# Attention and a three-way maxout layer on one core: the planner that orders all instructions gets new durations and lags

## The chip, the cores and the metric

One core of a Trainium2 chip runs the whole program. The metric is the device time of one execution in microseconds (us). A core has five engines with instruction queues of their own: TensorE (PE, matrix products; PEld in the profile is its loading of weights), VectorE (DVE), ScalarE (ACT), GpSimd (POOL) and SyncE (SP, which here only issues DMAs). Each engine takes its instructions strictly in the order in which they stand in its queue; an instruction that has to wait for another engine holds everything behind it.

## The reference

```python
def _attn_ref(q, k, v):                    # (8, 8, 576, 64) each
    scores = (1 / 8) * np.matmul(q, k.transpose(0, 1, 3, 2))
    mask = (pos[:, None] // 64) >= (pos[None, :] // 64)
    scores = np.where(mask, scores, -1e9)
    scores = scores - np.max(scores, axis=-1, keepdims=True)
    attn = np.exp(scores)
    attn = attn / (np.sum(attn, axis=-1, keepdims=True) + 1e-09)
    return np.matmul(attn, v)

def _moe_ref(x, w1, w2, w3, w_out):        # x: (4608, 512), w1..w3: (512, 768), w_out: (768, 512)
    h = np.maximum(np.maximum(x @ w1, x @ w2), x @ w3)
    return h @ w_out
```

So: attention over 8 batches of 8 heads with a mask in blocks of 64, its heads put side by side as the rows of x, three products of x with 512x768 matrices, their maximum, and a product with a 768x512 matrix, all in 32-bit floats.

## The kernel before

**Tiling.** Attention goes by pairs of heads: 4 pairs a batch. Batch 0 is cut in two parts, FRONT (queries 0 to 255) and BACK (the rest), so that its first results come early; the 28 pairs of batches 1 to 7 are whole. A pair needs: q and k loaded (tile nat, L875 and L893), turned (L824 on PE for batch 0, one DVE transpose L917 of 1152 columns for the others), scores on PE (L933, and L940 for the last 64 queries of both heads together), mask and row maximum in one DVE instruction (L422), exponential with row sum on ACT (L606, L960), reciprocal of the sum on DVE (L746, L750, L971, L977), normalising on ACT or POOL (L438, L440), turning the probabilities (PE L558 and L986 with copies for batch 0; for the others DVE L629 and L633 and then SP's DMAs L641, eight a pair), and the product with v (L1000). The result x is split in a rounded part xh (ACT, L249) and a remainder xl (POOL, L254), since the following products (L1118) work on 32-bit numbers in three steps: xh by the upper part of the weight, xl by the upper, xh by the lower. Each batch's x is one chunk of 256 columns and one of 320. A chunk takes 18 groups of 4 x 3 such products, the maximum on DVE (L1133), and then the output products L1184.

**Weights.** The 24 blocks of 512 columns ("units": 18 of w1 to w3, then 6 of w_out) are split into upper and lower part during the first 149 us. A unit is a DMA by POOL (L292), |w| on ACT (L302), five DVE operations in a row (L308, L315, L321, L327, L338; the first, second and fourth read one tensor, the other two read two), a rounding copy on ACT, three products on PE that add up what is left ("the whole": L345, L346, L347), and a copy back on ACT. There is one tile "left" that L338 writes and L347 reads.

**What sets the order.** The kernel first makes a list of jobs. A job has a rank, predecessors, buffers it takes and gives, and for each engine that could do it an assumed duration. `in_order` then plays this list through: at each moment an idle engine starts the ready job of lowest rank; a job becomes ready a lag (table LAG) after the last predecessor ends on another engine; buffers count. A job that two engines could do goes to whichever takes it first. The sequence so obtained is the order in which instructions are written to the queues of all engines, so assumed durations decide the order on each engine, and for some jobs the engine, but nothing else: the instructions themselves and their waits are the same.

The durations come from `pe`, `dve`, `act`, `pool` (functions of the columns), `norm_cost` (normalising), `RAISE` (a turn of 128 columns on PE), `SMALL` (a reciprocal or a sum of a few columns), and from sums of these in `Unit.__init__`, `Head.plan` and `Pair.plan4`; `GAP` is the time between two dependent DVE operations. DMA times (`SEND`, `LOAD`, `ASK`, `DMA`, `MOVE`, `TURNED`) are constants too.

Of the kernel before, what the change touches and what calls it, by code (L numbers as in the profile page):

```python
# [23 lines left out]
EPS = 1e-9  # L24


TO_PE = 250.0
LAG = {
    "PE": {"PE": 0.0, "ACT": 200.0, "DVE": 200.0, "POOL": 200.0, "SP": 200.0},
    "ACT": {"PE": TO_PE, "ACT": 0.0, "DVE": 90.0, "POOL": 160.0, "SP": 150.0},  # L30
    "DVE": {"PE": TO_PE, "ACT": 130.0, "DVE": 0.0, "POOL": 155.0, "SP": 150.0},
    "POOL": {"PE": TO_PE, "ACT": 130.0, "DVE": 130.0, "POOL": 0.0, "SP": 150.0},
    "SP": {"PE": 100.0, "ACT": 100.0, "DVE": 100.0, "POOL": 100.0, "SP": 0.0},
}
SEND = 620.0
# [3 lines left out]
MOVE = 4500.0  # L39
TURNED = 4400.0  # L40

GAP = 60.0
SMALL = 130.0

RAISE = 215.0
DEBUG = False


# [89 lines left out]
def pe(*cols, least=128):  # L138
    return sum(max(n, least) / 2.4 + 13.5 for n in cols)


def dve(n, fast=False):
    return 100.0 + n / (1.92 if fast else 0.96)


def act(n, psum=True):
    return (105.0 if psum else 135.0) + n / 1.2


def pool(n):  # L150
    return 120.0 + 2.6 * n


@with_exitstack
def kernel(
# [29 lines left out]
    TURN = 12  # L185
# [53 lines left out]
    def job(cost, rank, call, *args, after=(), take=(), give=(), lasts=0.0, moved=0.0):  # L239
        j = Job(cost, rank, lambda eng: call(eng, *args), after, take, give, lasts, moved)  # L240
        jobs.append(j)
        return j

    def join(after, give):
        return job({}, 0, lambda eng: None, after=after, give=give)
# [11 lines left out]
    class Unit:  # L257


        def __init__(self, u, src, dst, n, prior, *early, first=None):  # L260
            self.src, self.dst, self.n, self.u = src, dst, n, u
            self.last = n == DO
            rank = DELAY + PACE * u


            self.tag = f"wo{dst}" if self.last else f"w{u}"
            self.temps = (f"wo{u % NF}",) if not self.last else (f"wo{4 + dst % 2}",) if dst < 4 else ("osb", "osb")
            j = self.issued = job(
                {"POOL": ASK},
                rank - 8,  # L270
                self.load,
                after=(prior and prior.issued, first, *(e.sized for e in early if e)),
                take=(self.tag,) if self.last else (),
            )
            j = job({}, 0, lambda eng: None, after=(j,), lasts=MOVE, moved=1600.0)
            j = self.sized = job({"ACT": act(512, False)}, rank, self.size, after=(j,), take=self.temps)
            for step, fast in (
                (self.clamp, True),
                (self.shift, True),
                (self.sign, False),  # L280
                (self.power, True),
                (self.rest, False),
            ):
                c = dve(512, fast)
                j = job({"DVE": c}, rank, step, after=(j,), take=("left",) if step == self.rest else (), lasts=c + GAP)
            j = job({"ACT": act(512, False)}, rank, self.high, after=(j,))
            j = job({"PE": 6 * pe(512)}, rank, self.whole, after=(j,), take=("pm",), give=(*self.temps, "left"))
            self.done = job({"ACT": act(512)}, rank, self.lower, after=(j,), give=("pm",))
# [142 lines left out]
        return t.rearrange("p (k j r) -> p k j r", j=4, r=r)  # L431

    def norm_cost(n):
        return {"POOL": 160.0 + 1.86 * n, "ACT": 235.0 + n / 1.2}

    def normalise(eng, p, r):
        if eng == "ACT":
# [4 lines left out]
    class Head:  # L442
# [7 lines left out]
        def plan(self, t0):  # L450

            pair, part, self.exps, self.inv = self.pair, self.pair.part, {}, {}
            for n, ts in enumerate(part.groups):
                apart, r = None, t0 + (SECOND if part.beside and ts == part.later else n)
                for t in ts:
                    m = P * (t + 1)
                    d = job(
                        {"DVE": dve(m) + 120.0},
                        r + 1,
                        self.top,  # L460
                        t,
                        after=(pair.scored[ts], apart, pair.began),
                        take=("stat",) if pair.began is None else (),
                    )
                    pair.began = pair.began or d
                    if t != ts[-1]:
                        apart = job({}, 0, lambda eng: None, after=(d,), lasts=GAP)
                    self.exps[t] = job({"ACT": act(m) + 240.0}, r + 2, self.exp, t, after=(d,), take=(f"p{t}",))
                join([self.exps[t] for t in ts], BANK)

        def turns(self, t0, after):
# [9 lines left out]
            if part.last:  # L481
                first = job({"DVE": dve(512) + dve(128)}, t0 + 11, self.turn, 4, after=(pair.scaled, after), take=("pz",))
                self.turned = [first]
# [22 lines left out]
        def plain_turns(self, t0):  # L506
# [19 lines left out]
            for t in part.tiles:  # L526
                up = job(
                    {"PE": RAISE * (t + 1)},
                    t0 + 12,
# [8 lines left out]
            if part.last:  # L538
                if self.j == 0:
                    pair.raised = [  # L540
                        job({"PE": RAISE * n}, t0 + 12, pair.raise4, a, after=(pair.scaled, gate), take=("sb",))
                        for a, n in ((0, 4), (1, 1))
# [100 lines left out]
    BANK = ("sb", "sb5", "scores")  # L643

    class Pair:
# [12 lines left out]
        def plan(self, first, before):  # L658
# [67 lines left out]
            for r, ts in ((first + 7, [t for g in part.first for t in g]), (first + SECOND + 5, part.later)):  # L726
                if ts:
                    r = r if ts != part.later or part.beside else first + 8
                    cols = slice(min(COL[t] for t in ts), max(COL[t] for t in ts) + 1)
                    exps = [h.exps[t] for h in self.heads for t in ts]  # L730
                    inv = job({"DVE": SMALL}, r, self.sum, cols, after=exps, lasts=SMALL + GAP)
                    inv = job({"DVE": SMALL}, r, self.inverse, cols, after=(inv,))
                    for h in self.heads:
# [16 lines left out]
            nc.vector.reciprocal(rs[:, :, c], rs[:, :, c])  # L750

        def plan4(self, first, tq, last):
            asked = job({"ACT": 2 * act(64, False)}, first - TURN + 2, self.ask, after=(tq,), take=("q8",))
            tops = []
            for a in range(2):
                last = job({"PE": 4 * pe(64 if a else 512)}, first + 3 + a, self.qk4, a, after=(asked, last), take=BANK)
                tops.append(
                    job(
                        {"DVE": dve(64 if a else 512) + 120.0},
                        first + 4 + a,  # L760
                        self.top4,
                        a,
                        after=(last, *tops),
                        take=() if a else ("stat4",),
                    )
                )
            e = job({"ACT": act(512) + act(64) + 480.0}, first + 5, self.exp4, after=tops, take=("p4",), give=2 * BANK)
            inv = job({"DVE": SMALL}, first + 6, self.sum4, after=(e,), lasts=SMALL + GAP)
            inv = job({"DVE": SMALL}, first + 6, self.inverse4, after=(inv,))
            self.scaled = job(norm_cost(S), first + 7, self.scale4, after=(inv,), give=("stat4",))  # L770
            join((last,), ("q8",))
            return last
# [12 lines left out]
        def plain_qk(self, rank, loads):  # L785
# [13 lines left out]
            for n, (chunks, copies) in enumerate(banks):  # L799
                up = job(  # L800
                    {"PE": RAISE * len(chunks)},
                    rank,
# [5 lines left out]
                ) if n == 0 else job(  # L808
                    {"PE": RAISE * len(chunks)}, rank, self.raise_qk, n, chunks, after=(ups[0], loads["kn"], loads["qn"]), take=("sb", "sb5")
                )  # L810
# [28 lines left out]
        def finish(self, prior, r, priors={}):  # L839
            self.xjobs = {}  # L840
            for half in self.part.halves:
                n = HALF[half]
                done = job(
                    {"ACT": act(n), "DVE": dve(n)},
                    r + 2,
                    self.out,
                    half,
                    after=(priors.get(half, prior),),
                    take=(f"x32_{half}",),
                    give=("sb",),  # L850
                )
                h = job({"ACT": act(n, False)}, r + 4, self.x_high, half, after=(done,), take=(f"xh{half}",))
                self.xjobs[half] = job(
                    {"POOL": pool(n)}, r + 4, self.x_low, half, after=(h,), take=(f"xl{half}",), give=(f"x32_{half}",)
                )
            join((prior,), (self.tag,) * self.part.loads + ("vn",))
# [168 lines left out]
    left = {}  # L1025

    class Chunk:


        def __init__(self, b, half, pairs, prior, start, end):  # L1030
# [13 lines left out]
            for f in range(NF):  # L1044
                ev = None
                for i in range(3):
# [19 lines left out]
                    )  # L1066
                h = job({"ACT": act(256, False)}, NOW, self.high, f, after=(ev,), take=(f"hh{f}",))
                l = job({"POOL": pool(256)}, NOW, self.low, f, after=(h,))
                self.done[f] = [l]
                if spare:  # L1070
# [152 lines left out]
    rank = 0  # L1223
# [54 lines left out]
```

## Time and profile before

| what | us |
|---|---|
| three runs: median, lowest, highest | 927.47, 925.59, 927.82 |
| the profiled execution: time, span | 927.53, 925.7 |
| PE busy | 895.4 (97% of the span) |
| DVE busy | 530.1 (57%) |
| ACT busy | 479.6 (52%) |
| POOL busy | 246.3 (27%) |
| products L1118 on the chain that ended last | 49% of the span |
| output products L1184 on it | 16% |

A busy share is an average over the whole span; the windows below show it by stretch. A PE instruction's length in the profile contains a modelled end that overlaps the next one, so what an instruction costs PE is read from the distance of two starts, or from a run of equal ones on the chain of waits. The same holds for DVE and ACT, whose next instruction starts a little before the one ahead ends.

### The profile page before, as it was taken

What the parts mean: (1) busy time and instruction counts of PE and PEld (TensorE: products, weight loads), DVE (VectorE), ACT (ScalarE), POOL (GpSimd) and SP (SyncE); (2) the same over time, 40 slices, a digit from 0 to 9 for tenths busy, and PEclk for the clock granted to TensorE, in tenths of its full rate; (3) what the DMA queues carried; (4) which work ended last, traced back from release to release, by engine and by line L of the source; (5) the groups of instructions that cost most, each with busy time, mean ns of one, the idle gap of its engine ahead of it and who ended that gap; (6) DMA issues with size and microseconds to landing.
All of it is one profiled execution on the core that took longest, in us unless ns stands there. A gap on an engine that the chain in (4) does not pass through costs nothing.

```text
span 925.7 us, 16909 instructions
## 1 busy us (share of the span) xinstructions
PE 895.4 (97%) x5880; PEld 744.7 (80%) x5880; DVE 530.1 (57%) x1555; ACT 479.6 (52%) x1359; POOL 246.3 (27%) x377
## 2 busy tenths in 40 slices
PE   6798899999999999999999999999999999999998
PEld 4456667886988888888888888888888888899997
DVE  4999688786674655465574655465664655431101
ACT  3777557655564555556464555555464654522111
POOL 3522232333231222223132222223131322222101
PEclk9999999999999999999999999999999999999999
DMA  6841535576644554555533555555543543330010
GB/s 197 232 144 54 125 85 126 127 141 145 131 94 100 113 123 105 133 110 124 118 86 80 114 123 107 123 111 132 110 99 75 115 113 84 95 73 24 1 35 23
DMA packets 226132, 98.36 MB, mean 106 GB/s; under 512 B 189696, under 2 KB 218368, under 8 KB 226048
## 3 DMA queue, kind: packets, MB, share of 16 engines
q1 hardware_dynamic: 208192, 82.35, 40.3%
q0 software_dynamic: 3456, 12.58, 4.0%
q10 hardware_dynamic: 14400, 2.36, 1.4%
q8 instruction: 46, 0.75, 0.3%
q14 instruction: 38, 0.31, 0.1%
HBM read 41.94 MB, written 9.44 MB: 56 GB/s over the span
## 4 chain that ended last, share of the span: by engine, by line
PE 90%; DVE 5%; ACT 1%; issue 1%; DMA 1%; POOL 1%; ACTq 0%; SPq 0%; DVEq 0%; POOLq 0%
PE pm L1118 49%; PE pm L1184 16%; PE sb L1000 10%; PE sb L933 9%; PE sb L940 3%; PE pm L345 1%; DVE sb L422 1%; DVE wo L321 1%; DVE wo L308 1%; DVE left L338 1%; POOL p L440 1%; DMA nat<-in_q_dram 1%; PE sb L558 0%; ACT w L249 0%; DVE wo L315 0%
## 5 line engine op out<-in xcount | busy, mean ns | idle before, releaser
L1118 PE MATMUL pm<-xh,w 128*128 128x320 f32 (+1 forms) x2304 | 500.2, 304 | 0.7 <-ACT w L249 0.7
L1118 PEld LDWEIGHTS pm<-xh,w 128*128 128x128 f32 x2304 | 379.9, 190 | 20.1 <-issue 15.3
L1118 PE MATMUL pm<-xl,w 128*128 128x256 f32 (+1 forms) x1152 | 341.2, 296 | 0.7 <-POOL xl L254 0.5
L1118 PEld LDWEIGHTS pm<-xl,w 128*128 128x128 f32 x1152 | 219.0, 190 | 7.2 <-issue 5.3
L422 DVE CUSTOM_DVE_ANT_0 sb<-sb,mask 128x512 f32<-128x512 f32 (+3 forms) x288 | 144.8, 529 | 138.3 <-PE sb L940 70.0
L1133 DVE TENSOR_TENSOR m<-pm,m 128x256 f32<-128x256 f32 (+1 forms) x192 | 87.3, 455 | 167.1 <-PE pm L1118 159.0
L606 ACT ACTIVATE p<-sb,nm 128x128 f32<-128x128 f32 (+3 forms) x256 | 134.2, 528 | 75.0 <-DVE nm L422 62.8
L254 POOL TENSOR_TENSOR hl<-m,hh 128x256 fp32r<-128x256 f32 x96 | 71.6, 746 | 316.9 <-ACT hh L249 285.1
L629 DVE STREAM_TRANSPOSE pz<-p 128x512 f32<-128x512 f32 (+1 forms) x280 | 136.4, 525 | 21.8 <-ACT p L438 20.0
L440 POOL TENSOR_TENSOR p<-p,rs 128x384 f32<-128x384 f32 (+4 forms) x129 | 90.0, 719 | 186.7 <-DVE rs L750 180.8
L1184 PE MATMUL pm<-wo,hh 128*128 128x512 f32 x384 | 119.2, 391 | 0.0
L249 ACT CAST hh<-m 128x256 fp32r<-128x256 f32 x96 | 39.0, 406 | 121.3 <-DVE m L1133 120.7
L438 ACT ACTIVATE p<-p,rs 128x512 f32<-128x512 f32 (+4 forms) x159 | 89.6, 608 | 20.2 <-DVE rs L750 12.9
L1000 PE MATMUL sb<-pt,vn 128*64 128x320 f32 (+4 forms) x840 | 90.4, 362 | 4.0 <-ACT p L606 2.5
L254 POOL TENSOR_TENSOR xl<-x,xh 128x256 fp32r<-128x256 f32 (+1 forms) x64 | 51.9, 815 | 156.1 <-ACT xh L249 150.0
L933 PE MATMUL sb<-kq 64*128 64x256 f32 (+3 forms) x512 | 88.5, 466 | 2.6 <-DVE kq L251 2.0
L1000 PEld LDWEIGHTS sb<-pt,vn 128*64 128x64 f32 x840 | 55.3, 137 | 37.4 <-issue 5.0
L1184 PEld LDWEIGHTS pm<-wo,hh 128*128 128x128 f32 x384 | 71.0, 188 | 15.1 <-issue 0.3
L933 PEld LDWEIGHTS sb<-kq 64*128 64x128 f32 x512 | 45.5, 192 | 38.1 <-issue 21.7
L1184 PE MATMUL pm<-wo,hl 128*128 128x512 f32 x192 | 74.8, 390 | 0.0
L249 ACT COPY m<-pm 128x256 f32<-128x256 f32 (+1 forms) x96 | 38.3, 399 | 45.9 <-PE pm L1118 33.3
L249 ACT COPY osb<-pm 128x512 f32<-128x512 f32 x36 | 21.1, 587 | 75.7 <-PE pm L1184 75.7
(82 smaller groups left out, 762.5 us busy)
## 6 DMA issues: line engine op xcount, KB each, us to landing
pt<-pz SPq DMA_DIRECT2D x224, 200.0 KB, 3.9
w<-in_moe_w_dram POOLq DMA_DIRECT2D x18, 512.0 KB, 5.6
vn<-in_v_dram SPq DMA_DIRECT2D x64, 128.0 KB, 2.4
out_dram<-osb SPq DMA_DIRECT2D x32, 256.0 KB, 2.1
nat<-in_k_dram SPq DMA_DIRECT2D x112, 72.0 KB, 2.3
nat<-in_q_dram SPq DMA_DIRECT2D x96, 72.0 KB, 2.7
wo<-in_moe_w_out_dram POOLq DMA_DIRECT2D x6, 512.0 KB, 4.2
nat<-in_q_dram ACTq DMA_DIRECT2D x16, 72.0 KB, 3.2
```

The lines of the kernel that those rows point to most:

```text
L249: nc.scalar.copy(dst, src)
L254: {"DVE": nc.vector, "POOL": nc.gpsimd}[eng].tensor_tensor(out=dst, in0=a, in1=b, op=ALU.subtract)
L422: nc.vector.tensor_tensor_reduce(out=ps, in0=ps, in1=hidden, scale=-SCALE, scalar=first, op0=ALU.add, op1=ALU.min, accum_out=out_)
L438: nc.scalar.mul(p, p, r)
L440: nc.gpsimd.tensor_tensor(out=p, in0=p, in1=r.broadcast_to([P, p.shape[1]]), op=ALU.mult)
L606: nc.scalar.activation(dst, src, AF.Exp, bias=nm[:, c : c + 1], scale=-1.0, accum_out=sm[:, c : c + 1])
L629: nc.vector.transpose(dst, p[:, 0 : n * P])
L933: nc.tensor.matmul(ps, self.q[h.own, P * t : P * (t + 1)], self.k[h.own, 0:w], start=True, stop=True)
L1000: nc.tensor.matmul(o[h.own].rearrange("p (i u) -> p i u", u=n)[:, :, c0 : c0 + z - a], self.vn[:, kt, h.j, :], h.pt[:, :, h.off + a : h.of ...
L1118: nc.tensor.matmul(self.ps, w[i, f][:, c, :], xx, start=(c == 0 and s == 0), stop=(c == NC - 1 and s == 2))
L1133: nc.vector.tensor_tensor(out=m, in0=ps, in1=m, op=ALU.max)
L1184: nc.tensor.matmul(self.po[: self.rows], h, w[f], start=(f == 0 and s == 0), stop=(f == NF - 1 and s == 2))
```

## The change

New numbers in the planner, none in the instructions. The core of the diff:

```diff
-TO_PE = 250.0
+TO_PE = 180.0
-    "ACT": {"PE": TO_PE, "ACT": 0.0, "DVE": 90.0, "POOL": 160.0, "SP": 150.0},
-    "DVE": {"PE": TO_PE, "ACT": 130.0, "DVE": 0.0, "POOL": 155.0, "SP": 150.0},
-    "POOL": {"PE": TO_PE, "ACT": 130.0, "DVE": 130.0, "POOL": 0.0, "SP": 150.0},
+    "ACT": {"PE": TO_PE, "ACT": 0.0, "DVE": 140.0, "POOL": 180.0, "SP": 150.0},
+    "DVE": {"PE": TO_PE, "ACT": 120.0, "DVE": 0.0, "POOL": 240.0, "SP": 150.0},
+    "POOL": {"PE": TO_PE, "ACT": 90.0, "DVE": 130.0, "POOL": 0.0, "SP": 150.0},
-GAP = 60.0
-SMALL = 130.0
-RAISE = 215.0
+GAP = 85.0
+SMALL = 100.0
+RAISE = 110.0
 def dve(n, fast=False):
-    return 100.0 + n / (1.92 if fast else 0.96)
+    return 68.0 + n / (1.92 if fast else 0.96)
 def act(n, psum=True):
-    return (105.0 if psum else 135.0) + n / 1.2
+    return (52.0 if psum else 88.0) + n / 1.2
 def pool(n):
-    return 120.0 + 2.6 * n
+    return 150.0 + 2.15 * n
...
-                c = dve(512, fast)
+                c = dve(512, fast) + (130.0 if fast else 80.0)
...
-        return {"POOL": 160.0 + 1.86 * n, "ACT": 235.0 + n / 1.2}
+        return {"POOL": 250.0 + 1.5 * n, "ACT": 190.0 + n / 1.2}
...
-                        {"DVE": dve(m) + 120.0},
+                        {"DVE": dve(m) + 35.0},
-                    self.exps[t] = job({"ACT": act(m) + 240.0}, r + 2, self.exp, t, after=(d,), take=(f"p{t}",))
+                    self.exps[t] = job({"ACT": act(m) + 200.0}, r + 2, self.exp, t, after=(d,), take=(f"p{t}",))
```

The durations in `plan4` (L753 to L767) change in the same way. The new file has one line more from L286 on, so its L339 is L338 of before, its L918 is L917, and so on; the text uses the numbers of before.

What this does to the queues: on PE the two orders differ in the first tenth or so and then run through the same sequence of groups, with a few places exchanged; on DVE, ACT and POOL neighbouring instructions change places all the way, and POOL takes 27 normalisations of 512 columns where it took 15, and 11 of 576 where it took 3 (ACT the rest). Three places:

PE, a few rows from the start, where the third and the fourth pair of FRONT are turned (L824) and scored (L933); p_126 and its like are probabilities, pz the turned ones, vn is v. Before:

```order
L933 MATMUL sb<-kq 128x256 x2
L933 MATMUL sb<-kq 128x128 x2
L558 MATMUL sb<-plus,p_139 128x128 x2
L558 MATMUL sb<-plus,p_143 128x128
L824 MATMUL sb<-plus,nat 128x128 x4
L558 MATMUL sb<-plus,p_151 128x128 x2
L558 MATMUL sb<-plus,p_153 128x128
L1000 MATMUL sb<-pz,vn_75 64x256 x2
L1000 MATMUL sb<-pz,vn_75 64x4x32 x2
```

Now, in the same place:

```order
L559 MATMUL sb<-plus,p_126 128x128 x2
L559 MATMUL sb<-plus,p_143 128x128
L559 MATMUL sb<-plus,p_153 128x128
L934 MATMUL sb<-kq 128x256 x2
L934 MATMUL sb<-kq 128x128 x2
L559 MATMUL sb<-plus,p_151 128x128 x2
L1001 MATMUL sb<-pz,vn_75 64x256 x2
L1001 MATMUL sb<-pz,vn_75 64x4x32 x2
L825 MATMUL sb<-plus,nat 128x128 x4
```

The turns of the first pair's probabilities now stand ahead of the third pair's scores, and the first product with v ahead of the fourth pair's turn.

PE, around the 15th unit's whole (w_1024 before and w_1175 now are that unit's weights; kq is the turned q and k). Before, at row 201 of PE's order:

```order
L1118 MATMUL pm<-xl_271,w_697 128x256
L1118 MATMUL pm<-xh_265,w_697 128x256
L345 MATMUL pm<-wo_842,plus 128x512
L346 MATMUL pm<-w_1024,less 128x512
L347 MATMUL pm<-left,plus 128x512
```

Now, at row 256:

```order
L1119 MATMUL pm<-xl_331,w_989 128x256
L1119 MATMUL pm<-xh_326,w_989 128x256
L346 MATMUL pm<-wo_878,plus 128x512
L347 MATMUL pm<-w_1175,less 128x512
L348 MATMUL pm<-left,plus 128x512
L934 MATMUL sb<-kq 128x512 x2
```

Ahead of the 15th whole stand 138 products L1118 where 87 stood, and 26 more turns of 128 columns (L558, L824, L986).

DVE, around the second transpose of a whole pair's q and k (L917); left, w and wo are tiles of the weight units. Before:

```order
L338 SCALAR_TENSOR_TENSOR left<-wo_1179,wo_1264 128x512
L1133 TENSOR_TENSOR m<-pm,m 128x256
L308 TENSOR_SCALAR wo_1327<-wo_1327 128x512
L917 STREAM_TRANSPOSE kq<-nat 128x1152
L971 SCALAR_TENSOR_TENSOR rs_1319<-sm_1318 128x1
```

Now:

```order
L423 ISA sb,nm_1263<-sb,mask,nm_1263 128x64
L423 ISA nm_1263 128x1
L918 STREAM_TRANSPOSE kq<-nat 128x1152
L1134 TENSOR_TENSOR m<-pm,m 128x256
L339 SCALAR_TENSOR_TENSOR left<-w_870,wo_1023 128x512
L972 SCALAR_TENSOR_TENSOR rs_1265<-sm_1264 128x1
```

Before, this transpose stood behind the L338 of the 21st unit, now behind that of the 17th; the first such transpose stands 40 rows ahead of it before and 17 rows now.

## Rows read from the trace of the kernel before

**Rows 1.** Busy time by stretch: window, PE, PEld, DVE, ACT, POOL, clock, DMA, GB/s.
```profile
23.00:93.00 70.00, 59.16 (x317) 37.83 (x314) 66.21 (x163) 53.26 (x137) 25.22 (x33) 0.95 0.49 145
93.00:149.00 56.00, 51.20 (x310) 37.38 (x308) 41.69 (x106) 34.70 (x90) 17.86 (x23) 0.97 0.40 90
149.00:926.00 777.00, 771.03 (x5201) 660.14 (x5199) 411.84 (x1247) 383.06 (x1108) 195.01 (x302) 1.00 0.46 101
```

**Rows 2.** Waits of PE from 93 to 149 us: total, times, longest.
```profile
PE pm L346 <- ACT w L249: 2.7, 1, 2.7
```

**Rows 3.** Waits of DVE in that stretch.
```profile
DVE kq L917 <- DMA nat<-in_k_dram: 3.8, 1, 3.8
```

**Rows 4.** Chain of waits in order of time: start, length, what.
```profile
4.81 1.12 PE sb L824 x4
...
90.12 2.21 PE sb L1000 x20
...
92.87 0.86 PE sb L940 x2
...
95.98 1.07 PE pm L1118 x9
97.05 0.45 PE sb L824 x4
...
149.94 8.16 PE pm L1184 x36
```

**Rows 5.** PE in order of time: start, length, instruction.
```profile
94.95 0.79 PE L346 MATMUL pm<-w,less 128*128 128x512 f32 x1
...
96.89 0.93 PE L824 MATMUL sb<-plus,nat 128*128 128x128 f32 x7
```

**Rows 6.** PE from 207 to 220 us, products of 320 columns and what follows.
```profile
208.30 0.31 PE L1118 MATMUL pm<-xl,w 128*128 128x320 f32 x1
...
208.74 0.31 PE L1118 MATMUL pm<-xl,w 128*128 128x320 f32 x1
...
216.05 2.89 PE L1000 MATMUL sb<-pt,vn 128*64 128x320 f32 x26 [1.50 <-DMA pt<-pz]
218.88 0.70 PE L933 MATMUL sb<-kq 64*128 64x256 f32 x4
```

**Rows 7.** L346 on PE: shortest, median, longest; first and last start.
```profile
L346 PE MATMUL pm<-wo,less x6: 497/796/800, 112.9 to 148.9; 128*128 128x512 f32 x6
```

**Rows 8.** DVE in order of time.
```profile
85.91 0.42 DVE L1133 TENSOR_TENSOR m<-pm,m 128x256 f32<-128x256 f32 x1
...
88.38 0.69 DVE L422 CUSTOM_DVE_ANT_0 sb<-sb,mask 128x512 f32<-128x512 f32 x1
...
88.99 0.59 DVE L422 CUSTOM_DVE_ANT_0 sb<-sb,mask 128x384 f32<-128x384 f32 x1
...
89.50 0.73 DVE L422 CUSTOM_DVE_ANT_0 sb<-sb,mask 128x512 f32<-128x512 f32 x1
...
105.61 1.38 DVE L917 STREAM_TRANSPOSE kq<-nat 128x1152 f32<-128x1152 f32 x1 [3.77 <-DMA nat<-in_k_dram]
...
121.31 0.43 DVE L327 TENSOR_SCALAR wo<-wo 128x512 int32<-128x512 int32 x1
...
126.77 1.25 DVE L327 TENSOR_SCALAR wo<-wo 128x512 int32<-128x512 int32 x1
```

**Rows 9.** POOL beside the last of these.
```profile
126.15 1.59 POOL L440 TENSOR_TENSOR p<-p,rs 128x576 f32<-128x576 f32 x1
```

**Rows 10.** SP issues the moves of turned probabilities, two pairs.
```profile
206.34 6.51 SPq L641 DMA_DIRECT2D pt<-pz  x8
...
404.23 7.10 SPq L641 DMA_DIRECT2D pt<-pz  x8
```

**Rows 11.** PE where the second of these is used.
```profile
416.09 2.93 PE L1000 MATMUL sb<-pt,vn 128*64 128x320 f32 x28
```

**Rows 12.** All moves of L641, from issue to landing.
```profile
DMA to landing us min/median/max: 3.1/3.9/6.2
```

More of the change, by code (lines that the diff above doesn't have):

```diff
@@ L275, in __init__ @@
             j = job({}, 0, lambda eng: None, after=(j,), lasts=MOVE, moved=1600.0)
-            j = self.sized = job({"ACT": act(512, False)}, rank, self.size, after=(j,), take=self.temps)
+            j = self.sized = job({"ACT": act(512, False) + 65.0}, rank, self.size, after=(j,), take=self.temps)
             for step, fast in (
@@ L283, in __init__ @@
             ):
-                c = dve(512, fast)
-                j = job({"DVE": c}, rank, step, after=(j,), take=("left",) if step == self.rest else (), lasts=c + GAP)
+                c = dve(512, fast) + (130.0 if fast else 80.0)
+                e = "DVE"
+                j = job({e: c}, rank, step, after=(j,), take=("left",) if step == self.rest else (), lasts=c + GAP)
             j = job({"ACT": act(512, False)}, rank, self.high, after=(j,))
@@ L752, in plan4 @@
         def plan4(self, first, tq, last):
-            asked = job({"ACT": 2 * act(64, False)}, first - TURN + 2, self.ask, after=(tq,), take=("q8",))
+            asked = job({"ACT": 510.0}, first - TURN + 2, self.ask, after=(tq,), take=("q8",))
             tops = []
@@ L758, in plan4 @@
                     job(
-                        {"DVE": dve(64 if a else 512) + 120.0},
+                        {"DVE": dve(64 if a else 512) + 65.0},
                         first + 4 + a,
@@ L766, in plan4 @@
                 )
-            e = job({"ACT": act(512) + act(64) + 480.0}, first + 5, self.exp4, after=tops, take=("p4",), give=2 * BANK)
+            e = job({"ACT": act(512) + act(64) + 350.0}, first + 5, self.exp4, after=tops, take=("p4",), give=2 * BANK)
             inv = job({"DVE": SMALL}, first + 6, self.sum4, after=(e,), lasts=SMALL + GAP)
```

## The prediction

> **What bounds the kernel now.** I read the busy times by stretch first, since the 97% of PE are an average. From 149 us to the end PE is busy in 771.03 of 777 us [rows 1]: there the time is PE's work, and the order, which runs through the same groups there, can add to it but hardly take away. From 23 to 93 us DVE is busy in 66.21 of 70 us and PE's matmuls lie apart; from 93 to 149 us neither is full, DVE 41.69 of 56 us and PE 51.20 [rows 1]. So the span is this first stretch plus the PE work that is left when it ends, and an order gains by as much PE work as it gets done earlier in the stretch that DVE bounds. The waits say what PE lacks from 93 to 149 us: most of all the whole of a weight unit, 2.7 us in one piece, behind a DVE that stood 3.8 us for the load of q and k [rows 2, 3]. The prices of work come last: from the chain of waits, where equal instructions of PE stand in one piece, and from distances of starts.
>
> **Step 1, the work ahead of the 15th unit.** DVE paces the stretch and the weight units are its main work there, so I use a unit as the clock: what stands on PE and on DVE ahead of the 15th whole, before and now? Before, it started at 94.95 us [rows 5], where DVE's full stretch ends. Now 51 more products L1118 of 256 columns stand ahead of it on PE, 1.07/9 = 0.119 us each, 6.1 us, and 26 more turns at 0.45/4 = 0.11 us, 2.9 us [rows 4]; together 9.0 us of PE work. On DVE I count what stands ahead of the 15th L338: seven fewer weight operations of other units (some 0.43 to 0.6 us, 3.4 us less [rows 8]); two more row maxima of 512 and 384 columns, 88.99 - 88.38 = 0.61 and 89.50 - 88.99 = 0.51 us, and one of 64, 1.3 us in all; two more maxima L1133, 0.42 us each [rows 8]; copies and sums, 0.7 us more. Sum -0.6 us. If DVE is as full as before, the 15th whole comes 0.6 us earlier and PE has 9.0 us more behind it: a gain of 9.6 us. Where does it come from? The old numbers charged 0.75 us (100 + 512/0.96 + 120 ns) for a row maximum that takes 0.61, and 0.215 us for a turn that takes 0.11; played through with them, attention came later against the weight operations than DVE can really do it, and PE had fewer products ready per unit. It is no accident of the 15th: ahead of the 10th whole, PE has 7.5 us more and DVE 1.3 us less.
>
> **Step 2, from the 15th unit to the last.** The last whole began at 148.9 us [rows 7]. Ahead of the 24th L338 DVE now has 7.7 us more work (one more L917 at 1.38; seven more row maxima, 3.3; twelve transposes of probabilities, 3840 columns, which at L917's 1.38/1152 a column is an estimate of 4.6; two more L1133, 0.8; ten fewer copies net, small ones among them, some 2.4), 8.3 us more than at the 15th; PE has 13.5 us more (57 products of 320 columns, (208.74 - 208.30)/3 = 0.147 us each; 15 output products at 8.16/36 = 0.227; one group of scores at 0.70 and one pair's L940 at 0.86, with 0.11 for its last 64 columns, an estimate from the 512) [rows 4, 6], 4.5 us more than at the 15th. Were DVE full here, 8.3 - 4.5 = 3.8 us would be given back. It isn't: it was idle in 14.3 of the 56 us [rows 1], and that idle time covers the 8.3 us. I take nothing given back, and keep 3.8 for the range.
>
> **Step 3, the load of q and k.** The first L917 waits for a reload of nat that can start when PE's last turn L824 is through: that began at 96.89 us and L917 at 105.61 us, 8.7 us [rows 5, 8]. Before, DVE had some 5.7 us of work between the 15th unit's L338 and this transpose; now the turn stands behind the 13th whole, and DVE has about 12 us. So the 3.8 us stall should go, and with it up to 2.7 us of PE's wait; late next would be the POOL normalisation of the last 64 queries ahead of L986. But the second L917 now stands 6.6 us of DVE work behind the first one's start, where it was 16.5: 5.2 us after its end, against a reload that takes at most those 8.7. DVE then waits 0 to 3.5 us, with the L338 of the 18th unit behind it, and PE behind that; DVE has idle time here, PE has its lead. I take -1.5 us for the first and +0.5 for the second.
>
> **Step 4, the first products with v of batch 1.** At the fourth pair PE stood 1.50 us for the moved probabilities [rows 6]: SP's eight moves began at 206.34 and ended at 212.85 us, and a move lands 3.1 to 6.2 us after its issue [rows 10, 12]; there is no margin. Now the last scores of the second of these pairs stand 2.9 us of PE work later, and its product with v at the same place. So PE may wait 0 to 2.9 us more there; I take 1.5.
>
> **Step 5, the start.** The third pair's q goes to ACT's queue behind the first exponential, and its scores on PE behind three turns of probabilities, each about 0.28 us here, since L824 took 1.12 us for four [rows 4], at the lower of PE's two clock levels, not 0.11. That delays the third pair by about 1 us and brings the first product with v forward by 2 to 3. With fewer weight operations between, DVE may stand a little longer. Between -2 and +2 us; I take +0.5.
>
> **Step 6, POOL.** More normalisations of 512 and 576 columns move to POOL. A DVE operation beside one of these was slow: L327 took 1.25 us at 126.77 beside POOL's at 126.15, and 0.43 at 121.31 with POOL idle [rows 8, 9]. Ahead of the last weight load POOL has a net 896 columns more, 2.5 us at 1.59/576 a column, an estimate; so DVE loses 0 to 2.5 us more; I take 0.5, since half of this lies where DVE has idle time. [...]
>
> **The sum.** -9.6 - 1.5 + 0.5 + 1.5 + 0.5 + 0.5 = -8.1 us. It is made against the profiled execution's 927.53 us, 0.06 us from the median of the three runs: 919.4 us.
>
> **The rivals.** (a) *DVE never starves.* The lead of step 1 holds, the stall of step 3 goes wholly, and the new order, since its durations are nearer to the trace, has fewer waits in the 93 to 149 us: another 4 to 5 us of what PE stood idle (56 - 51.2 [rows 1]). 919.4 - 4.8 = 914.6 us, and 912 with the start at its good end. For it: 14.3 us of DVE idle time there. Against it: PE and DVE wait for one another in turn, which no duration cures.
>
> (b) *The lead is given back.* DVE is the bound up to the 24th unit (3.8 us of step 2), the second pair's product with v waits in full (2.9), the start costs 1.5: -9.6 + 8.2 = -1.4 us, 926.1 us. For it: 8.3 us more DVE work in a stretch where it is already busy 74% and stalls in order. Against it: in the b = 1 pairs the last transposes of probabilities stand 2 to 5 us of DVE work earlier than before.
>
> (c) *Slower: products with v wait in every batch.* POOL is slow at a normalisation (1.59 us for 576 columns [rows 9]) and gets more of the long ones, so the chain from scores to turned probabilities gets longer, while PE's places for scores and products with v stay. One pair in each batch has no slack: its eight moves began at 404.23 and ended at 411.33 us, with the median 3.9 the last landing is due at about 415.2, and the product began at 416.09 [rows 10 to 12]. If the moves come 3 us later in each of the six batches in which this recurs, PE waits 2.1 us in each, 12.6 us: 919.4 + 12.6 = 932 us. It decides from (8.1 + 2.8)/6 = 1.8 us of wait a batch on, 2.7 us of delay. For it: a margin of 0.9 us. Against it: the longer normalisations go to POOL in the order in which the planner found it free, and DVE's transposes keep their sequence.
>
> (d) *The order doesn't do what it says*, since the planner takes PE at its upper clock and the start runs at the lower: step 5 at its bad end, and 3 us more over the first units. 923 us; it stays faster, and counts with the forecast.
>
> **How the numbers follow.** Forecast 0.59, with a range of its own from 914.5 to 924.5 us (steps 3 to 6 at their good and at their bad ends in part); (a) 0.14; (b) 0.15; (c) 0.12. What a measurement of this kernel can tell from no change is about 0.3%, 2.8 us, so faster means under 924.7 us: 0.73, nearly all of the forecast and (a). Within 0.3%: 0.15, from (b). Slower: 0.12, from (c). The range leaves out the better half of (a) and most of (c): 911 to 928 us.
>
> **What would show it.** Right: the 15th whole starts near 94 us and PE has done 9 us more by then; no DVE wait of 3.8 us at the first L917; from the last whole on the chain of waits is PE alone, and what follows is as long as before less the lead. Wrong: weight wholes that come later by more than PE's extra work ahead of them (steps 1 and 2); a DVE stall of over 3 us at the second L917 (step 3); PE waits for moved probabilities at the first pairs of batch 1 (step 4) or once in every batch (c); a first product with v that is not earlier than at 20 us (step 5).

## The result, and the profile after

| | median us | lowest to highest | runs |
|---|---|---|---|
| before | 926.53 | 925.26 to 927.82 | 4 |
| changed | 913.76 | 911.82 to 914.20 | 4 |

The ratio is 0.9858 (95% interval 0.9836 to 0.988): 12.8 us less. The forecast was 8.1 us less, 919.4 us. The time lies in the range of 911 to 928 us, but below the forecast's own 914.5 to 924.5, next to the number of rival (a). The profiled executions, 927.53 and 913.83 us, have spans of 925.7 and 912.0 us; the accounts below are made between these, over 13.7 us.

The busy times by stretch, changed kernel (columns as in [rows 1]):

```profile
0.00:23.00 23.00, 14.15 (x63) 9.88 (x64) 9.81 (x39) 7.97 (x25) 8.94 (x23) 1.00 0.60 164
23.00:93.00 70.00, 67.38 (x389) 48.02 (x389) 66.22 (x168) 56.88 (x151) 33.55 (x41) 0.95 0.57 160
93.00:149.00 56.00, 52.94 (x306) 38.16 (x308) 47.51 (x128) 38.57 (x106) 12.54 (x17) 1.00 0.56 125
149.00:912.00 763.00, 758.38 (x5125) 647.04 (x5125) 405.71 (x1214) 368.29 (x1085) 199.78 (x302) 1.00 0.45 100
```

The one row of before that stands beside these and wasn't shown:

```profile
0.00:23.00 23.00, 14.04 (x62) 9.31 (x62) 10.36 (x42) 8.56 (x27) 8.23 (x20) 1.00 0.69 196
```

Read the first number behind the length, PE. In the first 23 us PE's busy time hardly changed. From 23 to 93 us PE is busy 8.2 us more than in [rows 1], while DVE is as full as before, to 0.01 us. From 93 to 149 us PE has 1.7 us more. So PE stands idle for 149 - 134.5 = 14.5 us of the first 149, where it was 24.6: 10.1 of the 13.7 us. Of the rest, 1.0 us is idle time of PE after 149 us (4.6 us for 5.7), and 2.6 us is PE's busy time over the whole span, 892.8 us for 895.4 with the same products.

The 15th and the last whole in PE's order of time (L347 is L346 of before):

```profile
95.26 0.80 PE L347 MATMUL pm<-w,less 128*128 128x512 f32 x1
...
150.07 0.80 PE L347 MATMUL pm<-wo,less 128*128 128x512 f32 x1
```

They start 0.3 and 1.2 us later than in [rows 5, 7], with 9.0 and 13.5 us more PE work ahead of them. Thus 8.7 us had been won at the 15th, and 12.3 at the last. PE's longest wait from 93 to 149 us and, behind the dots, all of its waits from there to the end:

```profile
PE pm L347 <- ACT w L249: 1.5, 1, 1.5
...
PE pm L1119 <- DMA nat<-in_k_dram: 0.5, 1, 0.5
PE pm L1119 <- ACT xh L249: 0.5, 1, 0.5
```

The 1.50 us before a product with v [rows 6] is gone, and none of its kind came. And the wait of [rows 3], now:

```profile
DVE kq L918 <- DMA nat<-in_q_dram: 2.4, 1, 2.4
```

It fell from 3.8 us, but now it is q that comes late. The chain shows the load's length:

```profile
91.03 0.51 ACTq L894
...
91.58 6.70 DMA nat<-in_q_dram
...
98.56 1.38 DVE kq L918
```

The second L918 has no wait in front of it:

```profile
106.21 1.38 DVE L918 STREAM_TRANSPOSE kq<-nat 128x1152 f32<-128x1152 f32 x1
```

### The profile page after: what moved, and what is told of

Same layout as the page of the kernel before. It is cut to its first block, busy times and chain, and to the rows that moved or that the text cites. A ratio compares the mean times of both kernels' runs of the same rounds, so it can differ in the third digit from the quotient of the medians.

```text
span 912.0 us, 16897 instructions
## 1 busy us (share of the span) xinstructions
PE 892.8 (98%) x5880; PEld 743.1 (81%) x5880; DVE 529.3 (58%) x1545; ACT 471.7 (52%) x1365; POOL 254.8 (28%) x381
## 4 chain that ended last, share of the span: by engine, by line
PE 90%; DVE 5%; DMA 1%; ACT 1%; issue 1%; ACTq 0%; POOL 0%; DVEq 0%
PE pm L1119 50%; PE pm L1185 16%; PE sb L1001 10%; PE sb L934 8%; PE sb L941 3%; PE pm L346 1%; DMA nat<-in_q_dram 1%; DVE sb L423 1%; DVE left L339 1%; DVE wo L322 1%; PE sb L559 1%; DMA nat<-in_k_dram 0%; DVE kq L251 0%; ACT p L439 0%; PE pm L348 0%
## 5 line engine op out<-in xcount | busy, mean ns | idle before, releaser
L607 ACT ACTIVATE p<-sb,nm 128x256 f32<-128x256 f32 (+3 forms) x256 | 133.9, 527 | 80.2 <-DVE nm L423 73.7
L441 POOL TENSOR_TENSOR p<-p,rs 128x128 f32<-128x128 f32 (+4 forms) x133 | 97.9, 755 | 253.9 <-DVE rs L751 194.5
L934 PE MATMUL sb<-kq 64*128 64x256 f32 (+3 forms) x512 | 89.1, 466 | 3.2 <-DVE kq L251 3.1
L1001 PE MATMUL sb<-pt,vn 128*64 128x320 f32 (+4 forms) x840 | 90.2, 363 | 0.4 <-DVE pt L251 0.3
L1001 PEld LDWEIGHTS sb<-pt,vn 128*64 128x64 f32 x840 | 55.1, 137 | 34.5 <-issue 1.7
L934 PEld LDWEIGHTS sb<-kq 64*128 64x128 f32 x512 | 46.3, 192 | 38.1 <-issue 20.8
```

The costliest lines, as they stand in the source:

```text
L441: nc.gpsimd.tensor_tensor(out=p, in0=p, in1=r.broadcast_to([P, p.shape[1]]), op=ALU.mult)
L607: nc.scalar.activation(dst, src, AF.Exp, bias=nm[:, c : c + 1], scale=-1.0, accum_out=sm[:, c : c + 1])
L934: nc.tensor.matmul(ps, self.q[h.own, P * t : P * (t + 1)], self.k[h.own, 0:w], start=True, stop=True)
L1001: nc.tensor.matmul(o[h.own].rearrange("p (i u) -> p i u", u=n)[:, :, c0 : c0 + z - a], self.vn[:, kt, h.j, :], h.pt[:, :, h.off + a : h.of ...
```

## The experiments

Times are medians; the ratio, and each gain below, is against runs of the kernel before on the same chip (925.56 us for the first four kernels tried, then 925.75, 926.70 and 927.72). What is said against the changed kernel goes by its median of 913.76 us; by the ratios these differences shift by up to 1.1 us. "PE idle" is 149 us less PE's busy time up to there in the profiled execution.

| run | us | ratio, 95% interval | PE idle, us | 15th, last whole at |
|---|---|---|---|---|
| before | 926.53 | | 24.6 | 94.95, 148.91 |
| changed | 913.76 | 0.9836 to 0.988 | 14.5 | 95.26, 150.07 |
| raise_alone | 920.18 | 0.9919 to 0.9965 | 17.9 | 98.87, 149.91 |
| all_but_raise | 917.84 | 0.9892 to 0.9936 | 18.5 | 87.08, 134.98 |
| dve_alone | 917.81 | 0.9893 to 0.992 | 17.0 | 86.41, 138.47 |
| dve_old | 921.21 | 0.993 to 0.996 | 19.8 | |
| act_pool_old | 918.23 | 0.9895 to 0.9931 | 18.5 | |
| lags_old | 912.74 | 0.9829 to 0.9864 | 13.6 | 95.44, 148.84 |
| units_260 | 917.78 | 0.9875 to 0.993 | 16.0 | |
| nosign_before | 918.87 | 0.9907 to 0.9954 | 19.5 | |
| nosign_after | 913.10 | 0.9831 to 0.9894 | 13.5 | |
| q_by_sync | 913.12 | 0.9841 to 0.9876 | 14.5 | |
| pe_fill | 911.42 | 0.9815 to 0.9857 | 14.6 | 91.82, 146.82 |
| combined | 908.26 | 0.9772 to 0.9821 | 11.8 | 92.38, 144.43 |

The theory at first was that of step 1, called the lead theory in the expectations: DVE paces the weight units, and the gain is PE work that the order puts ahead of them. The rivals were the truer durations as a whole, and a gain outside the first 149 us.

**The turn's number alone, and everything but it.**

The edit of raise_alone on the kernel before; all_but_raise is its reverse on the changed kernel:

```diff
-RAISE = 215.0
+RAISE = 110.0
```

> The kernel before with one number changed: RAISE 215 to 110. Lead theory (the gain is PE work that stands earlier against DVE's weight operations): in the order, PE has 6.1 us more work ahead of the 15th whole and 8.7 us more ahead of the last; DVE has 2.6 us more ahead of the 15th L338. Gain 8.7 - 2.6 = 6.1 us, about 920.5 us; the last whole no more than 3 us later than 148.9. Rival (it is the truer durations of all engines together, with fewer waits later on, and the turns are one of four parts): 2 to 3 us gained, about 924.

> The changed kernel with RAISE back at 215, all other new numbers kept. Lead theory: PE has the same work ahead of the 15th whole as in the kernel before (0.0 us) and 3.6 us less ahead of the last, DVE 1.1 us less ahead of the 15th L338; so between -1 and +3 us against the kernel before, about 927. Rival (truer durations of all engines): most of the gain stays, 916 to 919 us.

The first came out as the lead theory said: 5.4 us against 6.1. The second refutes it as the whole story: 7.7 us faster, where it allowed at most 1. PE has no more work ahead of the 15th whole than before, and yet this whole starts 7.9 us earlier:

```profile
87.08 0.80 PE L347 MATMUL pm<-w,less 128*128 128x512 f32 x1
```

From 23 to 93 us, raise_alone and all_but_raise in turn:

```profile
23.00:93.00 70.00, 63.69 (x352) 43.64 (x352) 66.95 (x170) 52.44 (x135) 33.10 (x39) 0.98 0.49 137
```

```profile
23.00:93.00 70.00, 62.63 (x346) 41.64 (x343) 67.66 (x176) 55.76 (x140) 28.44 (x35) 0.98 0.56 165
```

PE is busy 4.5 and 3.5 us more than before, 8.0 together, and the changed kernel has 8.2; the times add up as well, 5.4 + 7.7 = 13.1 against 12.8. So there are two sources of similar size. By the turn's number the 15th whole comes 3.9 us later and the last 1.0 us later, but with more attention and more products ahead of them, 6.1 and 8.7 us of PE work in the order. By the rest the same work stands ahead of them and is through earlier. What both do is to shorten PE's idle time.

**Is DVE's work the bound?** One operation of each unit is left out of both kernels, the order kept:

```diff
         def sign(self, eng):
             a = self.a.bitcast(I32)
-            nc.vector.scalar_tensor_tensor(
-                out=a, in0=self.high_word, scalar=-(2**30), in1=a, op0=ALU.bitwise_and, op1=ALU.bitwise_or
-            )
+            pass
```

> The kernel before, its order kept, with one DVE operation of each weight unit (L321, 0.68 us median, about 0.62 us from start to start) left out, so the weights lose their sign. Lead theory: DVE paces the kernel before up to the 15th whole, 14 x 0.62 = 8.7 us less DVE work ahead of it, and PE has 10.8 us from 23 to 93 and 4.8 from 93 to 149 us in which it stood; a gain of 7 us at least, 917 to 920 us. Rival (the start and the first 149 us are bounded by the chain between engines, not by DVE's work): less than 3 us.

> The changed kernel, its order kept, with the same DVE operation of each weight unit (now L322) left out, so the weights lose their sign. Lead theory: PE is now itself nearly full from 23 to 93 us (67.4 of 70) and from 93 to 149 us (52.9 of 56), so the same cut is worth at most 2.6 + 3.1 us and what the half clock costs: 2 to 5 us, 909 to 912 us, clearly less than the same cut gains on the kernel before. Rival (the gain of the change lies behind 149 us or in the chain between engines): the cut is worth the same on both kernels.

Before: 6.7 us faster, about as expected (917 to 920). Changed: 0.7 us by the medians and nothing by the ratios (0.9862 for 0.9858), where 2 to 5 were expected; the two intervals leave some 3.6 us either way, so it is nothing clear of the noise. The rival, the same worth in both kernels, fell: the difference between the two cuts is larger than their intervals allow for. The row of nosign_after:

```profile
23.00:93.00 70.00, 67.73 (x395) 48.65 (x396) 58.12 (x154) 57.35 (x151) 33.04 (x42) 0.95 0.59 165
```

DVE has 8.1 us less to do than in the changed kernel, and PE gains 0.35. In the changed kernel DVE is busy in 66.22 of 70 us, and yet 8.1 us less of its work gives PE next to nothing.

**Which of the other numbers.** dve_old, act_pool_old and lags_old put one group back in the changed kernel; dve_alone brings one group into the kernel before (lines between the changed ones are left out, marked by dots):

```diff
 dve_alone, on before
-GAP = 60.0
-SMALL = 130.0
+GAP = 85.0
+SMALL = 100.0
...
-    return 100.0 + n / (1.92 if fast else 0.96)
+    return 68.0 + n / (1.92 if fast else 0.96)
...
-                c = dve(512, fast)
+                c = dve(512, fast) + (130.0 if fast else 80.0)
...
-                        {"DVE": dve(m) + 120.0},
+                        {"DVE": dve(m) + 35.0},
...
-                        {"DVE": dve(64 if a else 512) + 120.0},
+                        {"DVE": dve(64 if a else 512) + 65.0},
```

> The changed kernel with the DVE numbers of before (base 100, row maximum + 120, no extra on weight operations, GAP 60, SMALL 130); RAISE, ACT, POOL and the lags new. New theory (two sources: the turn's number puts more PE work ahead of the weight wholes; the DVE numbers set weight operations against attention on DVE so that DVE and PE wait for each other less, which made the version without RAISE 8 us faster with no more PE work ahead): the second source goes, 919 to 921 us, like RAISE alone. Lead theory by counts alone: PE has 4.5 us less ahead of the last whole than in the changed kernel, DVE 0.7 us less: 917 to 918. Rival (the second source is in the ACT, POOL and lag numbers): 913 to 915.

> The changed kernel with the ACT and POOL numbers of before (their bases, norm_cost, the additions at the exponentials); RAISE, DVE and the lags new. New theory with the second source in the DVE numbers: PE has 3.2 us less ahead of the last whole than in the changed kernel, so 914 to 917 us. Rival (the second source is in the ACT and POOL numbers, which decide where a normalisation goes): 919 to 921.

> The kernel before with the DVE numbers of the changed one alone (base 68, row maximum + 35, weight operations + 130 and + 80, GAP 85, SMALL 100); RAISE, ACT, POOL and lags old. In the order, PE has the same work as before ahead of the 15th and of the last whole (0.0 us), DVE 0.7 us less and 3.0 us more. If the second source of the gain lies in the DVE numbers by themselves (undoing them in the changed kernel cost 7.4 us): 918 to 920 us, PE's idle time of the first 149 us down from 24.6 to about 18. If they act only together with the others, or only by counts: 924 to 927.

> The changed kernel with the lags of before (TO_PE 250 and the old table); all durations new. In the order, the work ahead of the 15th and the last whole stands within 0.3 us of the changed kernel's on PE and within 0.8 us on DVE. If the lags are no source of the gain: 913 to 915 us. If the parts each bear some (undoing the ACT and POOL numbers cost 4.4 us, the DVE numbers 7.4, the turn's number 4.1): 916 to 919.

The DVE numbers are the second source. Undone they cost 7.4 us (921.21, as the new theory had it); alone they give 8.9 us, somewhat more than everything but RAISE gives, with the same PE work ahead of the 15th and the last whole as before, which start 8.5 and 10.4 us earlier. Putting the old lags back costs nothing (912.74; the interval overlaps that of the changed kernel). The ACT and POOL numbers cost 4.5 us when undone, more than the 0 to 3 expected, though dve_alone does without them: the parts don't add here. The 15th whole of dve_alone, and where it wins:

```profile
86.41 0.80 PE L346 MATMUL pm<-w,less 128*128 128x512 f32 x1
```

```profile
23.00:93.00 70.00, 63.54 (x343) 41.41 (x343) 68.05 (x173) 53.38 (x133) 28.68 (x35) 0.98 0.56 165
93.00:149.00 56.00, 53.83 (x320) 39.28 (x320) 49.24 (x129) 37.34 (x101) 13.51 (x19) 1.00 0.46 105
```

PE 4.4 us more in the first and 2.6 us more in the second stretch, and DVE, which had stood 14.3 us from 93 to 149 us [rows 1], stands 6.8. That the DVE numbers set weight operations and row maxima in such turns that DVE and PE wait for one another less fits these rows, but it is argued and not shown: which of the DVE numbers and which exchange of neighbours does it was not tried.

**Further the same way.** Two of these three numbers go on in the direction of the change, TO_PE goes back (the cut is marked by dots):

```diff
-                c = dve(512, fast) + (130.0 if fast else 80.0)
+                c = dve(512, fast) + (260.0 if fast else 210.0)
...
-TO_PE = 180.0
+TO_PE = 220.0
...
-                    self.exps[t] = job({"ACT": act(m) + 200.0}, r + 2, self.exp, t, after=(d,), take=(f"p{t}",))
+                    self.exps[t] = job({"ACT": act(m) + 120.0}, r + 2, self.exp, t, after=(d,), take=(f"p{t}",))
```

> The changed kernel with three numbers pushed further the same way or against: each weight operation on DVE charged 260 and 210 ns on top where 130 and 80 stood, exponentials + 120 for + 200, TO_PE 220 for 180. In the order PE has 0.8 us more ahead of the last whole than in the changed kernel, DVE 5.3 us less ahead of the 15th L338 and 8.4 us less ahead of the last. If DVE still paces the first stretch: 909 to 912 us. If PE does (67.4 of 70 us busy in the changed kernel, and leaving out an operation of DVE gained nothing there): 912.5 to 914.5, the same.

A miss for both: 4 us slower than the changed kernel by the medians (the intervals just touch), with 0.8 us more PE work and 8.4 us less DVE work ahead of the last whole. Which of the three numbers did it, the run doesn't part. PE in order of time around its first whole:

```profile
27.57 1.11 PE L559 MATMUL sb<-plus,p 128*128 128x128 f32 x4 [1.89 <-ACT p L439]
...
33.44 0.80 PE L347 MATMUL pm<-w,less 128*128 128x512 f32 x1
```

The first whole comes at 33.44 (28.63 in the changed kernel), behind PE that waits 1.89 us for a normalisation. Work counted ahead of a point doesn't say how long PE stands before it. From 23 to 93 us of this run PE is busy in 65.1, DVE in 58.5 and ACT in 58.3 of 70 us, so none of them is full; that the idle time left comes of engines waiting for one another in turn is argued from this and not shown.

**The late load of q.**

```diff
-                queue = nc.scalar if eng == "ACT" else nc.sync
+                queue = nc.sync
```

> The changed kernel, order kept, with the loads of q of the whole pairs of batch 1 issued by SP's queue and not by ACT's, where the first of them stood behind an exponential (issued at 90.1 to 91.0 us, 2.3 us behind k's at 87.9). If the 2.4 us that DVE waits for q at its first L918, with 1.5 us of PE behind it, are on the path: the wait goes to about 1 us and the time to 912 to 913. If PE has the lead to cover it: 913.5 to 914, no change.

Inconclusive on what it was made for, since the wait stayed (2.34 us for 2.4):

```profile
98.34 1.38 DVE L918 STREAM_TRANSPOSE kq<-nat 128x1152 f32<-128x1152 f32 x1 [2.34 <-DMA nat<-in_q_dram]
```

The last of these loads was issued at 91.36 us where it had been 91.58, so the other queue hardly brought them forward, and the load takes 6.71 us from SP's queue as it took 6.70 from ACT's, while the median of all loads of q from SP's queue is 2.5 us in the changed kernel. What draws it out was not tried. It fits that the share of the 16 DMA engines (the last column but one) reads full, 1.11, in the changed kernel from 92 to 96 us, and nearly so, 0.96, before, from 100 to 104 us, ahead of the 3.8 us wait:

```profile
92.00:96.00 4.00, 3.38 (x21) 2.35 (x19) 3.96 (x9) 2.84 (x7) 1.49 (x2) 1.00 1.11 274
...
100.00:104.00 4.00, 4.00 (x30) 3.44 (x29) 1.16 (x2) 3.11 (x8) 0.00 (x0) 1.00 0.96 222
```

**PE kept busy at the start, and the three together.** In both kernels PE's granted clock is at half for a while in the first 149 us; the changed kernel's:

```profile
24.00:28.00 4.00, 3.21 (x13) 2.32 (x14) 3.66 (x16) 3.58 (x11) 1.19 (x3) 0.55 0.82 264
28.00:32.00 4.00, 4.00 (x14) 2.40 (x14) 2.95 (x7) 2.40 (x9) 2.77 (x4) 0.60 0.44 107
```

Before, it was three stretches:

```profile
32.00:36.00 4.00, 3.59 (x11) 1.86 (x12) 2.69 (x8) 3.45 (x10) 1.33 (x3) 0.57 0.82 218
56.00:60.00 4.00, 4.00 (x15) 2.73 (x14) 3.73 (x10) 3.23 (x11) 1.95 (x3) 0.57 0.73 239
128.00:132.00 4.00, 4.00 (x21) 3.76 (x19) 1.77 (x6) 0.93 (x2) 0.69 (x2) 0.57 0.79 186
```

So I put products that nobody reads where PE stands ahead of its first scores; `combined` is that, the lags of before and q by SP's queue.

```diff
+    def fill(n):
+        if n:
+            z = psm.tile([P, 512], F32, name="pm")
+            for _ in range(n):
+                nc.tensor.transpose(z[:, 0:P], plus.bitcast(F32), plus.bitcast(F32))
...
         def qk(self, eng, groups):
+            if self.b == 0 and self.part.loads == 1:
+                fill((2, 4, 0, 3)[self.hp])
```

and two more ahead of the first L559 (the lines below it move by up to 10: L825, L934, L1001 are L833, L944, L1011). The expectations speak of 13 products in five places; by the code and in the traces of both runs they are 11, in four.

> The changed kernel with 13 products of 128 columns that nobody reads, put on PE in five places before 22 us where it stood idle for 0.8 to 1.4 us, so that PE is busier ahead of the stretch at half clock (24.0 to 31.3 us in the profiled run; one run of the changed kernel had a mean clock of 1.000 and took 911.8 us, the three at 0.996 took 913.7 to 914.2). If idle time ahead of it brings the half clock on: no such stretch, 911 to 912.5 us in all runs. If it does not: 913.5 to 915, with the fillers in the way of the start.

> The changed kernel with three edits that each came out 0.6 to 2.3 us below its 913.8: the lags of before, q of the whole pairs of batch 1 loaded by SP's queue, and the 13 products that nobody reads ahead of 22 us. If what PE stands idle and what it runs at half clock in the first 149 us set the end, and the three take from different places: 913.8 - 1.0 - 0.6 - 2.3 = 909.9, so 909 to 911 us. If the three are within what the order's small exchanges give by chance: 911 to 914, as the changed kernel with the fillers alone.

pe_fill, 911.42 us, has no half clock between 20 and 44 us in its profiled execution, as expected. But two of its five executions lie within the 911 to 912.5 us expected of all, and the mean granted clock of the five goes from 0.994 to 0.999, so the half clock isn't gone from each; and its interval overlaps that of the changed kernel. combined, 908.26 us, lies under the 909 to 911 expected, and its interval lies clear below the changed kernel's: the fastest version. Its 1.6 us below the sum of its parts (909.9) are not clear of the noise of four measurements. PE's start, the changed kernel:

```profile
6.71 1.65 PE L934 MATMUL sb<-kq 64*128 64x256 f32 x8 [0.78 <-DVE kq L251]
...
10.84 1.65 PE L934 MATMUL sb<-kq 64*128 64x256 f32 x8 [1.44 <-DVE kq L251]
12.43 1.11 PE L825 MATMUL sb<-plus,nat 128*128 128x128 f32 x4
...
17.98 2.13 PE L1001 MATMUL sb<-pz,vn 128*64 128x256 f32 x8
...
22.01 0.92 PE L934 MATMUL sb<-kq 64*128 64x256 f32 x8 [0.87 <-DVE kq L251]
...
25.88 1.74 PE L1001 MATMUL sb<-pt,vn 128*64 128x256 f32 x8 [0.31 <-DVE pt L251]
...
28.63 1.42 PE L347 MATMUL pm<-w,less 128*128 128x512 f32 x1
```

and combined:

```profile
6.70 1.65 PE L944 MATMUL sb<-kq 64*128 64x256 f32 x8 [0.36 <-DVE kq L251]
...
10.84 0.92 PE L944 MATMUL sb<-kq 64*128 64x256 f32 x8 [0.58 <-DVE kq L251]
12.15 0.63 PE L833 MATMUL sb<-plus,nat 128*128 128x128 f32 x4 [0.39 <-PE sb L944]
...
15.88 0.87 PE L1011 MATMUL sb<-pz,vn 128*64 128x256 f32 x8
...
24.84 1.42 PE L347 MATMUL pm<-w,less 128*128 128x512 f32 x1
```

From 10.84 us on the same instructions take 0.92, 0.63 and 0.87 us for 1.65, 1.11 and 2.13, and the first whole comes 3.8 us earlier. How much of the gain is this and how much the half clock of 24 to 31 us, the runs don't part: combined has a half clock too in its profiled execution (mean clock 0.996, from 20 us on), while its other four executions have a mean of 1.000.

## Why the prediction was right, and where not

- **What bounds the kernel.** Right that the gain lies in PE work done earlier in the first 149 us: in the twelve kernels without fillers the span less PE's idle time up to 149 us is 897.5 to 901.1 us, while that idle time goes from 13.5 to 24.6. This account says where the time was won; by which numbers, the experiments say. Wrong that DVE was shown to be the pace by being full. Its work did count before (6.7 us for the cut, of some 8.7 us of DVE work ahead of the 15th whole), but the same 66.2 of 70 us stand in the changed kernel, where the cut gives nothing clear of the noise; and dve_alone gained 8.9 us with nearly the same work on DVE ahead of that whole.
- **Step 1**, -9.6 us: right in size, 8.2 us more PE busy by 93 us, 8.7 at the 15th whole. The argument holds for the turn's number. It failed for the DVE numbers: the work counted on DVE ahead of the 15th unit was 0.7 to 1.1 us less there, and the whole came 8 us earlier. That the count of the two together came so near the trace is therefore luck in part: the 9.0 us more of PE work ahead of the 15th whole cost hardly any time because the DVE numbers brought the wholes forward, not because a unit of DVE's work is a clock.
- **Step 2**, 0: right; nothing was given back, and DVE's idle time did cover its extra work (14.3 to 8.5 us).
- **Step 3**, -1.0 net: PE's busy time from 93 to 149 us rose by 1.7. The first stall shrank by 1.4 us and didn't go. The step took the reload as at most 8.7 us from the start of the turns; the turns (below) began at 86.90, and L918 at 98.56 us still had to wait for q, 11.7 us behind them, with a load of 6.70 us in it. The second L918, which was to wait up to 3.5, didn't.

```profile
86.90 0.93 PE L825 MATMUL sb<-plus,nat 128*128 128x128 f32 x7
```

- **Step 4**, +1.5: wrong. No product with v waits for moves any more; of PE's waits after 149 us the 1.50 is gone [rows 6], and two of 0.5 us are left, where one was; some 1.0 us less. Rival (c), built on the same thin margin, fell with it.
- **Step 5**, +0.5: about 0. The first product with v came 2.1 us earlier as said (17.98 against 20.13), the first whole 4.8 us later, and PE's busy time up to 23 us rose by 0.1.
- **Step 6**, +0.5: two DVE operations beside POOL's normalisations are slow in the changed kernel too, 1.09 and 1.43 us for 0.68 and 0.69 (below). What it costs the kernel was not tried; since 8.1 us less work on DVE gained nothing clear of the noise, I take it for little.
- **Left out of the sum:** the half clock. By the windows above it went from 3 x 4 x 0.43 = 5.2 us of lost clock to 4 x 0.45 + 4 x 0.40 = 3.4, at most 1.8 us of PE's work. The clock doesn't make the gain: at a mean granted clock of 0.996, executions of the kernel before took 923.8 to 926.7 us and those of the changed kernel 913.7 to 914.2; at 0.998, before 924.8 to 926.3, raise_alone 919.6 to 920.5, all_but_raise 917.0 to 918.3.

Together -8.2 - 1.7 - 1.0 - 0.1 - 1.8 = -12.8 of 13.7 us; 0.8 us of PE's shorter busy time stays open. What was mis-sized is the sum of steps 3 to 6 with +1.5 us, where the runs showed -2.8, and the clock beside it. Rival (a) had the time nearly (914.6) with a false reason: its 4 to 5 us were to come from 93 to 149 us and 1.7 did.

## What to carry to other kernels

An engine that is busy 95% of a stretch is not thereby its bound: leave out one of its operations and see, and account for a change of order by the idle time of the engine whose work sets the end, not by work counted ahead of a point. In a planner, try its numbers by groups: here one number and the DVE group gave 5.4 and 8.9 us alone, and the lags could be put back at no cost. Pushing the numbers on from there lost some 4 us.

## What the runs showed of the hardware

The level at which PE works at the start is read from durations, not from the column: up to 20 us the granted clock reads 1.00 in all windows, and yet eight products of scores take 1.65 us at 10.84, four turns 1.11 and eight products with v 2.13; in combined, with fillers ahead of them, 0.92, 0.63 and 0.87. The column reads 1.00 there because the trace has no record of the clock so early: its first record, at full, begins at 21.0 us in the changed kernel. Taken by half microseconds up to 149 us, the granted clock of the kernel before and of the changed one reads 1.00 or 0.50, with values between only where it changes. Read at 0.50 in the changed kernel, three turns take 0.88 us at 24.69 and eight products with v 1.74 at 25.88; read at 1.00, eight products of scores take 0.92 at 22.01 and four turns 0.60 at 41.74. So a turn takes 0.28 us at 12.43, 0.29 at 0.50 and 0.15 at 1.00, which fits the lower of the two levels at the start; the 2.13 us for the products with v are more than the 1.74 at 0.50, so not all of this is the clock.

What differs ahead is how long PE stood: 0.36 and 0.58 us in combined before its first two groups of scores, 0.78 and 1.44 in the changed kernel. That this sets the level is not shown: in pe_fill PE stood 0.36 and 0.28 us there, and its scores at 10.84 take 1.65.

DVE beside POOL, in the changed kernel, DVE and then POOL in order of time:

```profile
85.82 1.09 DVE L322 SCALAR_TENSOR_TENSOR wo<-w,wo 128x512 int32<-128x512 int32 x1
86.93 1.43 DVE L339 SCALAR_TENSOR_TENSOR left<-w,wo 128x512 fp32r<-128x512 uint32 x1
```

```profile
85.26 2.55 POOL L441 TENSOR_TENSOR p<-p,rs 128x512 f32<-128x512 f32 x2 [4.25 <-PE sb L1001]
```

Operations with two tensors to read take 0.68 to 0.69 us at the median (L322, L339); beside POOL's two normalisations they took 1.09 and 1.43. I had looked for this only at the fast operations with one tensor (L327, 0.43 and 1.25 us [rows 8]).
